# Two token blocks share the first layer's weights in three groups of the inner dimension instead of two, the weights' conversion follows a schedule over the steps, and the short token block comes third

## The chip, the cores and the metric

The program runs on one core of a Trainium2 chip. The metric is the device time of one execution in microseconds; lower is better. The core's engines are named as in the profile: PE multiplies matrices, PEld is its weight load, DVE and ACT do elementwise work, POOL is little used here, and SP issues the DMA transfers.

## The reference

Attention without a softmax (a decaying linear attention), then two feed-forward layers over its 2304 tokens of 512 features.

```python
scores = q @ k.T / sqrt(64)                    # 4 batches, 8 heads, 576 positions, heads of 64
gamma  = 1 - 2 ** (-5 - arange(8))             # per head
ret    = scores * where(i >= j, gamma ** (i - j), 0)
x      = (ret @ v)  -> (2304, 512)
h = x @ w_in;  g = where(h > 0, h, exp(min(h, 0)) - 1);  x = g @ w_out      # layer one, 2048 inner
h = maximum(x @ w_in2, 0);  out = (h * h) @ w_out2                            # layer two, 2048 inner
```

q, k and v are float32; the four weight matrices come as float64 (as pairs of 32-bit words).

## The kernel before

**Tokens and steps.** The 2304 tokens are cut into five blocks (`BLOCKS`, L24), four of 512 and one of 256. The inner dimension of 2048 is cut into 16 slices f of 128. A step is one block and one slice: `up` multiplies the block's x by w_in's slice (12 matmuls into one PSUM tile h), ACT and DVE make g of it, and `down1` or `down2`, called `LAG` = 2 steps later, multiplies g by w_out's slice (12 more for a block of 512, into four PSUM tiles acc). Every product is three matmuls, since each operand is split into an upper and a lower part (`split`, L108; `mm3`, L113). Layer one has 80 steps, layer two 80.

**Groups of layer one.** A block of 512 fills all four acc tiles, so only one block accumulates at a time. Blocks 0 and 1 share layer one's weights in two halves of f (`ORDER1`, L32): block 0 with f 0 to 7, block 1 with f 0 to 7, block 0 with f 8 to 15, block 1 with f 8 to 15. After a first half ACT copies acc out and SP stores it in DRAM (`parts`, L338, L340); at the end it is loaded back and DVE adds it (L322, L330). Then blocks 2 to 4 follow with 16 steps each.

**Attention.** A block's x is made of chunks of at most 128 positions. A chunk has three pieces (`attn_pieces`): transposes of q and k on PE, scores on PE with a mask on DVE (P, L239), values on PE with a split into x by ACT and DVE (L110, L111) and an update of the state st on DVE (L271). Before them DVE scales q and k (L198). Block 0's four chunks stand ahead of the steps; `SPREAD` (L35) says over which steps the pieces of each later block are given out. Block 1 has five chunks.

**Weights.** A unit is one slice of one matrix: 32 units per layer, in the order in which the steps need them (`units`, L362). A unit of layer one is loaded (L129, L134), converted to float32 by two ACT (L144, L145) and four DVE instructions (L146, L147, L148, L151), and split by one ACT and one DVE instruction. Before, `w1_step` (L404) does one unit per piece of block 0's attention and then two per step. Layer two's units are converted in layer one's later steps, parked in DRAM (`park_w`), and fetched and split when block 4 releases layer one's weights.

**What sets the order.** The program is traced in the order of the Python code, but a scheduler with a timeline of its own then fixes the order of the instructions on each engine, as their inputs become ready there. On the chip each engine takes its instructions strictly in that order and waits for semaphores. The SP queue does so too.

Of the kernel before, what the change touches and what calls it, by code (L numbers as in the profile page):

```python
# [14 lines left out]
ALU = mybir.AluOpType  # L15
# [5 lines left out]
KC = DM // P  # L21
NF = DFF // P
TB = 512
BLOCKS = [(0, 512), (512, 512), (1024, 512), (1536, 256), (1792, 512)]  # L24
NB = len(BLOCKS)
LAG = 2
WARM = 3

AHEAD = 6

HALF = NF // 2
ORDER1 = [(b, h * HALF + f) for h in range(2) for b in range(2) for f in range(HALF)]  # L32
ORDER1 += [(b, f) for b in range(2, NB) for f in range(NF)]

SPREAD = {1: (0, HALF - 1), 2: (3 * HALF, 4 * HALF - 1), 3: (2 * NF, 3 * NF - 3), 4: (3 * NF, 4 * NF - 3)}  # L35

MOST = float(np.array([0x7F7FF000 >> 3], np.uint32).view(np.float32)[0])

# [3 lines left out]
def chunks_of_blocks():  # L42


    out = []
    for t, n in BLOCKS:
        end, cs = t + n, []
# [35 lines left out]
def tile_kernel(ctx: ExitStack, tc, q, k, v, w_in1, w_out1, w_in2, w_out2, cst, out):  # L83
    nc = tc.nc
# [15 lines left out]
    parts = dram.tile([2, P, KC, TB], F32, tag="parts", name="parts")  # L100
    w2s = dram.tile([2 * NF, P, DM], F32, tag="w2s", name="w2s")
    x2s = [dram.tile([P, KC, 2, n], F32, tag=f"x2s{i}", name=f"x2s{i}") for i, (_, n) in enumerate(BLOCKS)]
    cs = const.tile([P, C_ALL], F32, name="cs")
# [4 lines left out]
    def split(pair_hi, pair_lo, src, eng=nc.vector):  # L108

        nc.scalar.copy(pair_hi, src)  # L110
        eng.tensor_tensor(out=pair_lo, in0=src, in1=pair_hi.bitcast(F32), op=ALU.subtract)  # L111

    def mm3(ps, l_hi, l_lo, r_hi, r_lo, first, last):  # L113
        nc.tensor.matmul(ps, l_hi, r_hi, start=first, stop=False)  # L114
        nc.tensor.matmul(ps, l_hi, r_lo, start=False, stop=False)  # L115
        nc.tensor.matmul(ps, l_lo, r_hi, start=False, stop=last)  # L116
# [85 lines left out]
    def attn_pieces(ch, blk):  # L202
        b, s, n = ch
        o = b * S + s - BLOCKS[blk][0]
        live = {}
# [77 lines left out]
    def up(layer, blk, f, mid):  # L283
        n = BLOCKS[blk][1]
        x = x_t[layer * NB + blk]
# [20 lines left out]
        split(g[:, 0, :n], g[:, 1, :n], t)  # L306
        g_t[blk, f] = g

    def halves(blk):
        return blk < 2  # L310

    def down1(blk, f):
        n = BLOCKS[blk][1]
        g, w = g_t.pop((blk, f)), w_t[0, 1, f]
        half = halves(blk)
        first, last = f == 0 or half and f == HALF, f == NF - 1 or half and f == HALF - 1
        if first:
            acc_t[blk] = [ps_acc.tile([P, TB], F32, tag="acc", name=f"acc{m}") for m in range(KC)]
        if f == NF - 1 and half:
            back = [raw_p.tile([P, 2, TB], F32, tag="raw", name="part") for _ in range(KC // 2)]  # L320
            for i, t in enumerate(back):
                nc.sync.dma_start(out=t, in_=parts[blk, :, 2 * i:2 * i + 2])  # L322
        for m in range(KC):
            c = slice(m * P, (m + 1) * P)
            a = acc_t[blk][m][:, :n]
            mm3(a, w[:, 0, c], w[:, 1, c], g[:, 0, :n], g[:, 1, :n], first, last)
            if f == NF - 1:
                if half:
                    t = back[m // 2][:, m % 2]
                    nc.vector.tensor_tensor(out=t, in0=a, in1=t, op=ALU.add)  # L330
                    a = t
                x2 = g_p.tile([P, 2, TB], F32R, tag="g", name="x2")[:, :, :n]
                split(x2[:, 0], x2[:, 1], a)
                nc.sync.dma_start(out=x2s[blk][:, m], in_=x2.bitcast(F32))
            elif last:
                if m % 2 == 0:
                    part = raw_p.tile([P, 2, TB], F32, tag="raw", name="part")
                nc.scalar.copy(part[:, m % 2], a)  # L338
                if m % 2:
                    nc.sync.dma_start(out=parts[blk, :, m - 1:m + 1], in_=part)  # L340

    def down2(blk, f):
        t0, n = BLOCKS[blk]
# [19 lines left out]
    w1 = [(0, *u) for u in units]  # L363
    w2 = [(1, *u) for u in units]
# [7 lines left out]
    at = dict(load=0, scale=0, next=0, raw=0, f32=0, split=0, raw2=0, f322=0, park=0, fetch=0, split2=0)  # L372
# [28 lines left out]
            work(todo_[at[name]])  # L401
            at[name] += 1

    def w1_step(n):  # L404

        for _ in range(n):
            while at["raw"] < min(at["f32"] + AHEAD, len(w1)):
                step("raw", 99, w1, lambda u: load_raw(*u))
            step("split", at["f32"], w1, split_w)
            step("f32", at["raw"], w1, to_f32)  # L410
# [3 lines left out]
    first = [attn_pieces(ch, 0) for ch in blocks[0]]  # L414
# [6 lines left out]
    load_next()  # L421
    scale_next()
    scale_next()
    for c, piece in ((0, 0), (1, 0), (0, 1), (1, 1), (0, 2), (2, 0), (1, 2), (3, 0), (2, 1), (3, 1), (2, 2), (3, 2)):
        first[c][piece]()
        w1_step(1)
        if piece == 0 and c < 2:
            scale_next()
        if (c, piece) in ((0, 2), (2, 2)):
            load_next()  # L430
    scale_next()
    at["next"] = len(first)
    steps = [(0, blk, f) for blk, f in ORDER1]
    steps += [(1, blk, f) for blk in range(NB) for f in range(NF)]
    pend = []
    for i, (layer, blk, f) in enumerate(steps):
        def mid():
            for of, (lo, hi) in SPREAD.items():
                if lo <= i < hi:
                    need = 3 * len(blocks[of])  # L440
                    for _ in range((i - lo + 1) * need // (hi - lo) - (i - lo) * need // (hi - lo)):
                        attn_step()
            if at["split"] < len(w1):
                w1_step(2)
            elif layer == 0 and i >= NF and at["f322"] < min(len(w2), (i - NF + 1) * 0.7):

                step("park", at["f322"], w2, park_w)
                with tc.issue_after(mark[0]):
                    step("f322", at["raw2"], w2, to_f32)
                while at["raw2"] < min(len(w2), at["f322"] + 2):  # L450
                    step("raw2", 99, w2, lambda u: load_raw(*u))

        up(layer, blk, f, mid)
        pend.append((layer, blk, f))
        if len(pend) > LAG:
            l, bb, ff = pend.pop(0)
            (down1, down2)[l](bb, ff)
        if at["f322"] == len(w2):
            step("park", 99, w2, park_w)

        j = i - (NB - 1) * NF
        if j >= 0:
            while at["split2"] < len(w2):
                _, which, ff = w2[at["split2"]]
                if ff + (LAG if which else 0) > j:
                    break
                while at["fetch"] < min(at["split2"] + 4, len(w2)):
                    step("fetch", 99, w2, fetch_w)
                step("split2", 99, w2, split_w)

        if (layer, f) == (0, 1) and blk == NB - 1 or (layer, f) == (1, LAG) and blk < NB - 1:
            n = blk + 1 if layer else 0
            new_x(NB + n)
            nc.sync.dma_start(out=x_t[NB + n].bitcast(F32)[:, :, :, :BLOCKS[n][1]], in_=x2s[n])
# [28 lines left out]
```

## Time and profile before

| | |
|---|---|
| median of 3 runs | 934.76 us (933.84 to 935.75) |
| profiled execution | 936.7 us |
| its span, first to last instruction | 934.9 us |
| mean granted PE clock | 0.979 |
| PE busy | 903.4 us (97%), 4934 matmuls |
| DVE busy | 503.0 us (54%) |
| ACT busy | 425.0 us (45%) |
| DMA | 93.27 MB, mean 100 GB/s |

A busy time counts an instruction from its start to its end; on PE, DVE and ACT neighbours overlap, so a stretch in which an engine is called full may still have differing numbers of instructions in it. How far apart two starts are is then the better measure. The granted clock is that of PE, as a share of full speed; it has two levels, 1.2 and 2.4 GHz, and a stretch's mean lies between.

### The profile page before, as it was taken

How to read it: one execution, taken by the hardware profiler on the slowest of the kernel's cores; microseconds unless marked ns; L12 is line 12 of the kernel's file. 1: busy time of each engine (PE TensorE's matmuls, PEld its weight loads, DVE VectorE, ACT ScalarE, POOL GpSimd, SP SyncE). 2: the span in 40 equal slices, each digit the busy share in tenths (PEclk: the TensorE clock that was granted, in tenths of full speed). 3: DMA queues.
4: the chain of work that ended last, by engine and by line, in shares of the span. 5: the costliest groups of instructions: out<-in, count | busy, mean ns of one | idle time of the engine just before them, and what ended most of it. 6: DMA issues, size and time to landing. Idle time of an engine off the chain costs nothing.

```text
span 934.9 us, 12416 instructions
## 1 busy us (share of the span) xinstructions
PE 903.4 (97%) x4934; PEld 751.9 (80%) x4934; DVE 503.0 (54%) x882; ACT 425.0 (45%) x770; POOL 9.3 (1%) x12
## 2 busy tenths in 40 slices
PE   8799679999999999999999999999999999999997
PEld 5677568888787788899888888888888888898886
DVE  5899997367866766788566632222222222323222
ACT  3788554466645555666566632222222222322221
POOL 3000000000000000000000000000000000000000
PEclk9799869999999999999999999999999999999999
DMA  9993621052842833573533520030002001100001
GB/s 233 313 363 80 169 46 23 1 174 90 255 121 72 251 128 96 180 215 103 181 102 102 168 90 1 1 126 9 1 1 90 1 0 60 77 1 22 1 1 45
DMA packets 95929, 93.27 MB, mean 100 GB/s; under 512 B 59136, under 2 KB 77696, under 8 KB 95360
## 3 DMA queue, kind: packets, MB, share of 16 engines
q1 hardware_dynamic: 95872, 92.49, 32.5%
q8 instruction: 38, 0.62, 0.3%
q14 instruction: 19, 0.16, 0.1%
HBM read 67.84 MB, written 24.64 MB: 99 GB/s over the span
## 4 chain that ended last, share of the span: by engine, by line
PE 88%; DVE 9%; DMA 1%; issue 1%; ACT 0%; SPq 0%; DVEq 0%
PE acc L114 14%; PE h L114 14%; PE h L115 13%; PE acc L115 13%; PE h L116 13%; PE acc L116 13%; PE ps_o L255 2%; DVE f L148 1%; PE ps_s L236 1%; DVE f L151 1%; PE ps_o L251 1%; PE ps_t L223 1%; DVE w L111 1%; DVE f L146 1%; DMA v<-in_v_dram 1%
## 5 line engine op out<-in xcount | busy, mean ns | idle before, releaser
L114 PE MATMUL h<-x,w 128*128 128x512 f32 (+1 forms) x640 | 240.3, 376 | 2.8 <-DVE t L301 2.5
L115 PE MATMUL h<-x,w 128*128 128x512 f32 (+1 forms) x640 | 239.1, 374 | 1.2 <-DVE x L111 1.2
L116 PE MATMUL h<-x,w 128*128 128x512 f32 (+1 forms) x640 | 238.1, 372 | 0.0
L305 DVE SCALAR_TENSOR_TENSOR t<-h,t 128x512 f32<-128x512 f32 (+1 forms) x80 | 51.1, 638 | 230.0 <-ACT t L303 230.0
L303 ACT ACTIVATE t<-h 128x512 f32<-128x512 f32 (+1 forms) x80 | 44.4, 555 | 237.2 <-PE h L116 237.2
L114 PEld LDWEIGHTS h<-x,w 128*128 128x128 f32 x640 | 121.9, 191 | 25.6 <-DVE t L301 3.6
L115 PEld LDWEIGHTS h<-x,w 128*128 128x128 f32 x640 | 121.9, 190 | 23.5 <-DVE x L111 2.6
L110 ACT CAST g<-t 128x512 fp32r<-128x512 f32 (+1 forms) x160 | 92.1, 577 | 103.2 <-DVE t L305 52.1
L116 PEld LDWEIGHTS h<-x,w 128*128 128x128 f32 x640 | 122.2, 191 | 20.8
L111 DVE TENSOR_TENSOR g<-t,g 128x512 fp32r<-128x512 f32 (+1 forms) x160 | 101.8, 637 | 65.1 <-ACT g L110 58.6
L115 PE MATMUL acc<-g,w 128*128 128x512 f32 (+1 forms) x320 | 118.4, 371 | 1.1 <-DVE g L111 1.1
L116 PE MATMUL acc<-g,w 128*128 128x512 f32 (+1 forms) x320 | 118.1, 370 | 0.0
L114 PE MATMUL acc<-g,w 128*128 128x512 f32 (+1 forms) x320 | 112.4, 376 | 0.0
L114 PE MATMUL acc<-w,g 128*128 128x512 f32 x288 | 112.3, 390 | 0.0
L115 PE MATMUL acc<-w,g 128*128 128x512 f32 x288 | 112.3, 390 | 0.0
L116 PE MATMUL acc<-w,g 128*128 128x512 f32 x288 | 111.6, 389 | 0.0
L300 DVE SCALAR_TENSOR_TENSOR t<-e,t 128x512 f32<-128x512 f32 (+1 forms) x80 | 50.9, 636 | 57.7 <-ACT t L298 57.3
L296 ACT ACTIVATE t<-h 128x512 f32<-128x512 f32 (+1 forms) x80 | 44.4, 555 | 76.3 <-PE h L116 72.1
L115 PEld LDWEIGHTS acc<-g,w 128*128 128x128 f32 x320 | 60.3, 189 | 11.5 <-DVE g L111 1.6
L114 PEld LDWEIGHTS acc<-g,w 128*128 128x128 f32 x320 | 59.6, 188 | 11.4 <-DVE x L111 0.5
L116 PEld LDWEIGHTS acc<-g,w 128*128 128x128 f32 x320 | 60.3, 188 | 10.2
L116 PEld LDWEIGHTS acc<-w,g 128*128 128x128 f32 x288 | 54.1, 188 | 11.3
(65 smaller groups left out, 922.4 us busy)
## 6 DMA issues: line engine op xcount, KB each, us to landing
raw<-in_moe_w_in_dram SPq DMA_DIRECT2D x32, 512.0 KB, 6.1
raw<-in_moe_w_out_dram SPq DMA_DIRECT2D x32, 512.0 KB, 5.8
w2s<-f SPq DMA_DIRECT2D x32, 256.0 KB, 2.2
x2s<-x SPq DMA_DIRECT2D x16, 512.0 KB, 3.3
f<-w2s SPq DMA_DIRECT2D x32, 256.0 KB, 2.6
x<-x2s SPq DMA_DIRECT2D x4, 2048.0 KB, 7.8
out_dram<-o SPq DMA_DIRECT2D x18, 256.0 KB, 2.7
q<-in_q_dram SPq DMA_DIRECT2D x13, 256.0 KB, 4.9
```

What stands on the lines that cost most here:

```text
L110: nc.scalar.copy(pair_hi, src)
L111: eng.tensor_tensor(out=pair_lo, in0=src, in1=pair_hi.bitcast(F32), op=ALU.subtract)
L114: nc.tensor.matmul(ps, l_hi, r_hi, start=first, stop=False)
L115: nc.tensor.matmul(ps, l_hi, r_lo, start=False, stop=False)
L116: nc.tensor.matmul(ps, l_lo, r_hi, start=False, stop=last)
L146: nc.vector.tensor_scalar_min(a, a, MOST)
L148: nc.vector.scalar_tensor_tensor(out=ai, in0=upper, scalar=-(1 << 31), in1=ai, op0=ALU.bitwise_and, op1=ALU.bitwise_or)
L255: nc.tensor.matmul(ps[e * D:(e + 1) * D, p, :n], vn[:n, 2 * p + e, :], live[e][:n, p, :n], start=not s, stop=True, skip_group_check=True,)
L296: nc.scalar.activation(t, h, AF.Relu, scale=-1.0)
L300: nc.vector.scalar_tensor_tensor(out=t, in0=e, scalar=1.0, in1=t, op0=ALU.add, op1=ALU.mult)
L303: nc.scalar.activation(t, h, AF.Relu)
L305: nc.vector.scalar_tensor_tensor(out=t, in0=h, scalar=0.0, in1=t, op0=ALU.max, op1=ALU.mult)
```

## The change

The short block moves from fourth to third place: block 2 has 256 tokens and two chunks of attention, block 3 has 512 tokens and five chunks. Blocks 0 and 1 go through three groups of f (0 to 5, 6 to 10, 11 to 15) instead of two halves. The middle group adds its sum to the one loaded back and stores it again. `SPREAD` gives block 1's pieces to steps 0 to 4 (before: 0 to 6). `w1_to` takes the number of units that are to be split by then, from the table `EARLY` during block 0's attention and from `units1` at each step, and layer two's conversion starts at step 32 (before: after layer one's, from step 16) at the pace of `units2`.

```diff
--- before.py
+++ after.py
@@ -21,18 +21,34 @@
 KC = DM // P
 NF = DFF // P
 TB = 512
-BLOCKS = [(0, 512), (512, 512), (1024, 512), (1536, 256), (1792, 512)]
+BLOCKS = [(0, 512), (512, 512), (1024, 256), (1280, 512), (1792, 512)]
 NB = len(BLOCKS)
 LAG = 2
 WARM = 3
 
 AHEAD = 6
 
-HALF = NF // 2
-ORDER1 = [(b, h * HALF + f) for h in range(2) for b in range(2) for f in range(HALF)]
+
+GROUPS = ((0, 6), (6, 11), (11, 16))
+ORDER1 = [(b, f) for lo, hi in GROUPS for b in range(2) for f in range(lo, hi)]
+SHARED = len(ORDER1)
 ORDER1 += [(b, f) for b in range(2, NB) for f in range(NF)]
 
-SPREAD = {1: (0, HALF - 1), 2: (3 * HALF, 4 * HALF - 1), 3: (2 * NF, 3 * NF - 3), 4: (3 * NF, 4 * NF - 3)}
+SPREAD = {1: (0, 5), 2: (SHARED - 5, SHARED - 1), 3: (SHARED, SHARED + NF - 2), 4: (SHARED + NF, SHARED + 2 * NF - 2)}
+
+EARLY = (0, 0, 0, 1, 1, 2, 3, 4, 5, 6, 6, 7)
+
+
+def units1(i):
+    return 7 + 1.4 * min(i + 1, 5) + 0.85 * max(i - 4, 0)
+
+
+def units2(i):
+
+    i -= SHARED - 1
+    return 0.6 * min(i, NF) + max(i - NF, 0)
+
+
 
 MOST = float(np.array([0x7F7FF000 >> 3], np.uint32).view(np.float32)[0])
 
@@ -306,17 +322,16 @@
         split(g[:, 0, :n], g[:, 1, :n], t)
         g_t[blk, f] = g
 
-    def halves(blk):
-        return blk < 2
-
     def down1(blk, f):
         n = BLOCKS[blk][1]
         g, w = g_t.pop((blk, f)), w_t[0, 1, f]
-        half = halves(blk)
-        first, last = f == 0 or half and f == HALF, f == NF - 1 or half and f == HALF - 1
+        shared = blk < 2
+        first, last = (any(f == r[e] - (e == 1) for r in (GROUPS if shared else ((0, NF),))) for e in range(2))
         if first:
             acc_t[blk] = [ps_acc.tile([P, TB], F32, tag="acc", name=f"acc{m}") for m in range(KC)]
-        if f == NF - 1 and half:
+
+        more = shared and last and f >= GROUPS[0][1]
+        if more:
             back = [raw_p.tile([P, 2, TB], F32, tag="raw", name="part") for _ in range(KC // 2)]
             for i, t in enumerate(back):
                 nc.sync.dma_start(out=t, in_=parts[blk, :, 2 * i:2 * i + 2])
@@ -324,20 +339,23 @@
             c = slice(m * P, (m + 1) * P)
             a = acc_t[blk][m][:, :n]
             mm3(a, w[:, 0, c], w[:, 1, c], g[:, 0, :n], g[:, 1, :n], first, last)
+            if not last:
+                continue
+            if more:
+                part = back[m // 2]
+                nc.vector.tensor_tensor(out=part[:, m % 2], in0=a, in1=part[:, m % 2], op=ALU.add)
+                a = part[:, m % 2]
             if f == NF - 1:
-                if half:
-                    t = back[m // 2][:, m % 2]
-                    nc.vector.tensor_tensor(out=t, in0=a, in1=t, op=ALU.add)
-                    a = t
                 x2 = g_p.tile([P, 2, TB], F32R, tag="g", name="x2")[:, :, :n]
                 split(x2[:, 0], x2[:, 1], a)
                 nc.sync.dma_start(out=x2s[blk][:, m], in_=x2.bitcast(F32))
-            elif last:
+                continue
+            if not more:
                 if m % 2 == 0:
                     part = raw_p.tile([P, 2, TB], F32, tag="raw", name="part")
                 nc.scalar.copy(part[:, m % 2], a)
-                if m % 2:
-                    nc.sync.dma_start(out=parts[blk, :, m - 1:m + 1], in_=part)
+            if m % 2:
+                nc.sync.dma_start(out=parts[blk, :, m - 1:m + 1], in_=part)
 
     def down2(blk, f):
         t0, n = BLOCKS[blk]
@@ -401,9 +419,9 @@
             work(todo_[at[name]])
             at[name] += 1
 
-    def w1_step(n):
-
-        for _ in range(n):
+    def w1_to(n):
+
+        while at["split"] < min(int(n), len(w1)):
             while at["raw"] < min(at["f32"] + AHEAD, len(w1)):
                 step("raw", 99, w1, lambda u: load_raw(*u))
             step("split", at["f32"], w1, split_w)
@@ -421,9 +439,10 @@
     load_next()
     scale_next()
     scale_next()
-    for c, piece in ((0, 0), (1, 0), (0, 1), (1, 1), (0, 2), (2, 0), (1, 2), (3, 0), (2, 1), (3, 1), (2, 2), (3, 2)):
+    pieces = ((0, 0), (1, 0), (0, 1), (1, 1), (0, 2), (2, 0), (1, 2), (3, 0), (2, 1), (3, 1), (2, 2), (3, 2))
+    for (c, piece), n in zip(pieces, EARLY):
         first[c][piece]()
-        w1_step(1)
+        w1_to(n)
         if piece == 0 and c < 2:
             scale_next()
         if (c, piece) in ((0, 2), (2, 2)):
@@ -441,8 +460,8 @@
                     for _ in range((i - lo + 1) * need // (hi - lo) - (i - lo) * need // (hi - lo)):
                         attn_step()
             if at["split"] < len(w1):
-                w1_step(2)
-            elif layer == 0 and i >= NF and at["f322"] < min(len(w2), (i - NF + 1) * 0.7):
+                w1_to(units1(i))
+            elif layer == 0 and i >= SHARED and at["f322"] < min(len(w2), units2(i)):
 
                 step("park", at["f322"], w2, park_w)
                 with tc.issue_after(mark[0]):
```

The order on the engines, at three places. First DVE, about the last write of block 1's x (the row with x_528 before, x_480 after); w0_12 is the split of slice 12 of w_in, w1_11 that of slice 11 of w_out, f_ a unit in conversion, raw_ its loaded words. Before:

```order
L146 TENSOR_SCALAR f_1175<-f_1175 128x512
L148 SCALAR_TENSOR_TENSOR f_1163<-raw_837,f_1163 128x512
L147 TENSOR_SCALAR f_1175<-f_1175 128x512
L111 TENSOR_TENSOR w0_12_1160<-f_1054,w0_12_1160 128x512
L151 ISA f_1163<-raw_837,f_1163 128x1024
L111 TENSOR_TENSOR x_528<-ps_o_1126,x_528 128x4x64
L148 SCALAR_TENSOR_TENSOR f_1175<-raw_930,f_1175 128x512
L271 TENSOR_TENSOR st_101<-ps_u_1141,st_101 64x4x64 x2
L146 TENSOR_SCALAR f_1222<-f_1222 128x512
L111 TENSOR_TENSOR w1_11_1172<-f_1163,w1_11_1172 128x512
```

After:

```order
L167 ISA f_1490<-raw_1203,f_1490 128x1024
L162 TENSOR_SCALAR f_1537<-f_1537 128x512
L127 TENSOR_TENSOR w1_10_1487<-f_1439,w1_10_1487 128x512
L163 TENSOR_SCALAR f_1537<-f_1537 128x512
L127 TENSOR_TENSOR w0_12_1534<-f_1490,w0_12_1534 128x512
L164 SCALAR_TENSOR_TENSOR f_1537<-raw_1250,f_1537 128x512
L162 TENSOR_SCALAR f_1584<-f_1584 128x512
L127 TENSOR_TENSOR x_480<-ps_o_924,x_480 128x4x64
L167 ISA f_1537<-raw_1250,f_1537 128x1024
L162 TENSOR_SCALAR f_1676<-f_1676 128x512
```

The split of w0_12 stands a few rows ahead of the last x in both; the rows about it are the same kinds of work.

Second PE, where the last attention piece of block 1 (ps_o, ps_u) ends and block 1's first two steps begin (h). Before, with the 96 products of 8 steps of block 0 in `up` and as many in `down1` ahead of it:

```order
L255 MATMUL ps_o<-P_1122,v 64x64
L255 MATMUL ps_o<-P_1120,v 64x64
L255 MATMUL ps_o<-P_1122,v 64x64
L265 MATMUL ps_u<-v,k 64x64 x8
L114 MATMUL h<-x,w_0_189 128x512
L114 MATMUL h<-x,w_1_217 128x512
L115 MATMUL h<-x,w_0_189 128x512
L116 MATMUL h<-x,w_0_189 128x512
```

After, with 72 and 72 of 6 steps ahead of it:

```order
L271 MATMUL ps_o<-P_920,v 64x64
L271 MATMUL ps_o<-P_918,v 64x64
L271 MATMUL ps_o<-P_920,v 64x64
L281 MATMUL ps_u<-v,k 64x64 x8
L130 MATMUL h<-x,w_0_217 128x512
L130 MATMUL h<-x,w_1_269 128x512
L131 MATMUL h<-x,w_0_217 128x512
L132 MATMUL h<-x,w_0_217 128x512
```

The rows are alike; the steps of block 0 in front of them are two fewer.

Third SP, the transfers issued while block 1's attention runs: q_, k_, v_ are inputs of chunks, parts_93 the partial sums in DRAM, raw_16.. units of layer two. Before:

```order
L188 DMA q_910<-in_q_dram 64x8x64
L188 DMA k_912<-in_k_dram 64x8x64
L188 DMA v_914<-in_v_dram 64x8x64
L129 DMA raw_1609<-in_moe2_w_in_dram 128x4x256
L340 DMA parts_93<-part_1356 128x1024
L188 DMA q_1031<-in_q_dram 128x8x64
L340 DMA parts_93<-part_1366 128x1024
L129 DMA raw_1611<-in_moe2_w_in_dram 128x4x256
L134 DMA raw_1655<-in_moe2_w_out_dram 128x1024
L188 DMA k_1033<-in_k_dram 128x8x64
L188 DMA v_1035<-in_v_dram 128x8x64
```

After:

```order
L204 DMA q_619<-in_q_dram 128x8x64
L204 DMA k_621<-in_k_dram 128x8x64
L204 DMA v_623<-in_v_dram 128x8x64
L204 DMA q_716<-in_q_dram 64x8x64
L358 DMA parts_93<-part_1116 128x1024
L358 DMA parts_93<-part_1126 128x1024
L204 DMA k_718<-in_k_dram 64x8x64
L204 DMA v_720<-in_v_dram 64x8x64
L204 DMA q_841<-in_q_dram 128x8x64
L204 DMA k_843<-in_k_dram 128x8x64
```

Two stores of partial sums now stand in front of the k of block 1's last chunk (k_718; k_912 before), and layer two's units are gone from here.

## Rows read from the trace of the kernel before

**Rows 1.** Stretches: busy us (x instructions) by engine, granted clock, DMA share, GB/s.

```profile
core 0: us, PE busy (x) PEld busy (x) DVE busy (x) ACT busy (x) POOL busy (x), PEclk, DMA share, GB/s
...
100.00:120.00 20.00, 10.04 (x95) 8.53 (x94) 19.89 (x40) 10.69 (x20) 0.00 (x0) 0.75 0.68 191
...
125.00:131.00 6.00, 5.69 (x14) 4.51 (x15) 5.96 (x13) 2.60 (x6) 0.00 (x0) 0.54 0.33 70
...
137.00:141.00 4.00, 3.89 (x10) 3.08 (x11) 4.00 (x9) 1.61 (x3) 0.00 (x0) 0.57 0.01 1
...
157.00:200.00 43.00, 43.00 (x204) 35.15 (x203) 21.75 (x35) 24.98 (x43) 0.00 (x0) 1.00 0.09 31
...
280.00:300.00 20.00, 18.82 (x125) 15.40 (x124) 11.10 (x21) 12.05 (x21) 0.00 (x0) 1.00 0.19 49
...
380.00:450.00 70.00, 70.00 (x634) 66.16 (x633) 52.65 (x113) 43.78 (x100) 0.00 (x0) 1.00 0.56 176
```

**Rows 2.** PE's timeline, block 1's attention: start, us, instruction, [idle before it <-releaser].

```profile
119.36 1.97 PE L251 MATMUL ps_o<-qT,st 128*128 128x64 f32 x8 [3.13 <-DVE P L239]
```

**Rows 3.** PE's timeline from block 1's first step on.

```profile
125.31 0.79 PE L115 MATMUL h<-x,w 128*128 128x512 f32 x1 [0.67 <-DVE x L111]
...
125.90 0.63 PE L116 MATMUL h<-x,w 128*128 128x512 f32 x1
...
126.33 0.63 PE L114 MATMUL h<-x,w 128*128 128x512 f32 x1
...
132.88 0.60 PE L223 MATMUL ps_t<-cs,q 128*128 128x128 f32 x4
...
133.32 0.60 PE L223 MATMUL ps_t<-cs,k 128*128 128x128 f32 x4
...
135.25 1.16 PE L236 MATMUL ps_s<-qT,kT 64*128 64x128 f32 x16 [1.34 <-ACT kT L228]
...
137.11 0.61 PE L114 MATMUL h<-x,w 128*128 128x512 f32 x1 [0.69 <-DVE t L301]
...
142.47 1.05 PE L251 MATMUL ps_o<-qT,st 128*128 128x128 f32 x8
...
143.46 1.09 PE L255 MATMUL ps_o<-P,v 128*64 128x128 f32 x16
```

**Rows 4.** DVE's groups by line, 38.2 to 125.3 us: busy us, mean ns, idle.

```profile
L111 DVE TENSOR_TENSOR w<-f,w 128x512 fp32r<-128x512 f32 x21 | 14.2, 683 | 0.1
...
L146 DVE TENSOR_SCALAR f<-f 128x512 f32<-128x512 f32 x21 | 8.8, 418 | 0.0
...
L300 DVE SCALAR_TENSOR_TENSOR t<-e,t 128x512 f32<-128x512 f32 x8 | 5.5, 684 | 1.8 <-ACT t L298 1.8
```

**Rows 5.** DVE's timeline, three neighbours in the full stretch.

```profile
102.46 0.41 DVE L147 TENSOR_SCALAR f<-f 128x512 int32<-128x512 int32 x1
102.79 1.28 DVE L148 SCALAR_TENSOR_TENSOR f<-raw,f 128x512 int32<-128x512 int32 x2
104.00 0.68 DVE L111 TENSOR_TENSOR w<-f,w 128x512 fp32r<-128x512 f32 x1
```

**Rows 6.** DVE's timeline: last x of block 0, DVE's one wait, last x of block 1.

```profile
38.26 0.69 DVE L111 TENSOR_TENSOR x<-ps_o,x 128x512 fp32r<-128x512 f32 x1
...
62.63 0.69 DVE L300 SCALAR_TENSOR_TENSOR t<-e,t 128x512 f32<-128x512 f32 x1 [1.83 <-ACT t L298]
...
124.85 0.41 DVE L111 TENSOR_TENSOR x<-ps_o,x 128x256 fp32r<-128x256 f32 x1
```

**Rows 7.** ACT's timeline: first activation of h in steps 12, 15 and 16.

```profile
156.99 0.60 ACT L296 ACTIVATE t<-h 128x512 f32<-128x512 f32 x1 [3.58 <-PE h L116]
...
174.62 0.60 ACT L296 ACTIVATE t<-h 128x512 f32<-128x512 f32 x1 [1.41 <-PE h L116]
...
180.06 0.60 ACT L296 ACTIVATE t<-h 128x512 f32<-128x512 f32 x1 [1.41 <-PE h L116]
```

**Rows 8.** The page's DMA issues: count, KB each, median us to landing.

```profile
q<-in_q_dram SPq DMA_DIRECT2D x13, 256.0 KB, 4.9
```

## The prediction, made before the changed kernel ran

> **What bounds the kernel now.** I read a table of stretches first, then the timelines of PE, DVE and ACT where a stretch looks odd, then DVE's groups by line. The page calls PE busy nearly throughout; the table of stretches [rows 1] shows two regimes under that. From 157 us on PE is filled at full clock (157:200 and 380:450 have PE 43.00 of 43 and 70.00 of 70 us); only 280:300 loses 1.2 us. A 512-token step takes 5.44 us there, from one activation of h to the next [rows 7], so its 24 matmuls start 0.227 us apart. Before 157 us DVE sets the pace: in 100:120 it works 19.89 of 20 us, PE 10.04, at a granted clock of 0.75. The PE timeline [rows 2] shows the attention of block 1 waiting for DVE's masking (3.13 us for P of its last chunk). The gate is block 1's x: PE cannot finish block 1's first step until DVE has written the last piece of it, at 124.85 us [rows 6]; block 0's last piece was at 38.26. So the kernel is a DVE-bound front and a PE-bound rest, and the change pays by when PE is released, and by how much dense work PE has then done.
>
> **DVE in front of the gate.** DVE's instructions overlap, so their price is the distance of their starts: 0.60 us for 512 columns (two L148 take 102.79 to 104.00), 0.33 for a tensor-scalar [rows 5]. The lines of that stretch [rows 4] show what fills it: 21 weight splits, 21 tensor-scalars of each kind, 8 steps of ELU, and the rest of conversions, scalings and masks. By program order 162 DVE instructions stand after block 0's last x up to block 1's; at these prices 83.7 us, against 86.6 measured (the difference is one wait of 1.83 us for ACT at 62.63 [rows 6] and small ones). In the changed program 154 stand there: the ELU of two steps less (6 instructions, 3.6 us), two scalings less (1.2), one L151 and one tensor-scalar less (0.9), two state updates more (0.8). That is 4.9 us less. The weight splits are 21 in both. The pacing says 14 units by step 4, but the order in which DVE got them is the scheduler's: when block 1's last x comes, the changed DVE has split w0_12, which its steps first read at step 23. So the conversions stay in front of the gate, and it opens at 125.3 - 4.9 = 120.4 us. Bounds: 1.8 us earlier, if the wait for ACT does not recur (the order has other DVE work at hand there); 2 us later, because k of block 1's last chunk is now queued on SP behind two stores of partial sums, which wait for step 5's accumulators, and a load of this kind takes 4.9 us to land in the median [rows 8]. I take neither.
>
> **PE in front of the gate.** Before, block 0 runs 8 steps of its first group before block 1 is needed; now 6. Two steps, 48 matmuls at 0.227 us, 10.9 us of dense work, move from where PE had time to spare to behind the gate. Nothing takes their place: the attention pieces in front are the same, and PE waits for DVE that much longer. This is the main term, +10.9.
>
> **Behind the gate.** Before, PE needs from 125.31 to 156.99, where step 12's activation starts [rows 7], 31.7 us, for 82 dense matmuls (18.6 us) and 5.4 us of attention (by the starts in [rows 3]: four groups of transposes at 0.44, one and a half times scores at 1.1, values at 2.0). So 7.7 us are lost. Of these 4.2 are the slow clock: 12 matmuls start 0.43 us apart instead of 0.227 [rows 3], and 9 more from 137.11 on, the stretches whose mean clocks are 0.54 and 0.57 [rows 1]. The rest is waiting, 1.34 and 0.69 us [rows 3] and little ones, because DVE still has 30 us of work against PE's 24. Now PE has 34.9 us there and DVE 34.6 (64 instructions instead of 56), so PE should wait less. I take 4.0 us lost: 2.4 for the first slow stretch and 1.6 of waits; bounds 0 and 7.7. By program order both engines have done the same work by step 12 in both kernels, so the sum up to there is -4.9 + 10.9 + (4.0 - 7.7) = +2.3 us; with the bounds of the loss -1.7 to +6.0, with those of the gate as well -3.5 to +8.0.
>
> A rule of the Trainium skill speaks on the clock here: "TensorE: Matmul & The Clock Gate", section "HAM oscillation — how this bites in real kernels", says that PE work which follows a long wait begins throttled, and pays for it again after each such wait. This trace agrees (0.43 us a matmul behind the gate). By the rule the longer hole ends in a slow start again and the sum is +2.3; without it the sum would be -0.1.
>
> **The rest of the program.** The third group adds a pass of partial sums per block: 8 DVE adds of 128x512 (8 x 0.60 = 4.8 us) and 4 MB of transfers, in steps 16 to 26, where DVE works 21.75 of 43 us and DMA has a share of 0.09 [rows 1]: nothing; if that cover were gone, at most 4.8 us. Layer two's conversions leave steps 16 to 31; PE was full there, so -0.4 (0 to -1). The short block, now third, carries five chunks of attention and block 1's final sums: 56.7 us of DVE work by the same prices, against 48.6 for the short block before, in a stage that took some 69 us with PE full (in 380:450 [rows 1]). The order crowds it at its start (21 us of DVE against 16 of PE over four steps). In 280:300 PE lost 1.2 us; I take +1.0, bounds 0 and 4, half of the added DVE work. Layer two's products are the same matmuls in another order of blocks: 0.
>
> **The sum.** The profiled execution took 936.7 us, its span 934.9. The change gives +2.3 - 0.4 + 1.0 = +2.9, so 939.6 for an execution like that one. It lies 1.9 above the median of the runs, 934.76; on that scale the forecast is 937.7 us.
>
> **Rivals.** First, the change comes out faster, because the DVE front loses its wait and the hole closes at once. The gate then opens at 118.6, PE runs its 34.9 us without slow clock or waits, and the short block costs nothing: -4.9 - 1.8 + 10.9 - 7.7 - 0.4 = -3.9, about 931 us. For it: PE now has as much work as DVE behind the gate, so DVE can hide. Against it: the clock was low after each hole before, and this hole is longer. It decides where the gate opens early and less than 2 us are lost behind it. Second, no change: 0 to 3 us are lost behind the gate instead of 4, the rest as forecast, 933 to 936.6 us. Third, the pacing does what it says on the engine: 12 units fewer in front of the gate, each 2.5 us of DVE, up to 30 us off the gate, and PE loses little of 20 us: the order of DVE says no, so I count it within the first. Fourth, the short block in third place becomes DVE-bound and its whole +4 is paid, with 7.7 lost behind the gate: -4.9 + 10.9 - 0.4 + 4 = +9.6, 944 us. Against it: 56.7 us of DVE in 69.
>
> **Chances.** Forecast, later by 2 to 6 us: 0.46; its own range is 936.6 to 941. Faster: 0.21. No change: 0.22. The fourth: 0.11. For 8 in 10 the range takes in most of the faster rival and of the fourth: 930.5 to 945. About 0.2% (1.9 us) is what a measurement of this kernel can tell from no change; faster by more 0.21, within 0.22, slower by more 0.57.
>
> **What would show it.** In the profile after: block 1's last x on DVE 4 to 5 us earlier than 124.85; PE idle or slow from about 85 to 121 us, longer than before; step 12's activation near 159 instead of 157, and equal distances from then on. If block 1's last x comes before 116, my count of DVE is wrong; if step 12 is reached before 157, my loss behind the gate is; if steps 32 to 47 show PE waits of several us, the fourth rival is right. Dense steps at other than 5.44 us would overturn all of it.

## The result, and the profile after

The changed kernel takes 945.38 us in the median of 4 runs (942.22 to 946.56); the kernel before, beside it, 935.25 (933.84 to 935.98, 4 runs). The ratio is 1.0105, with a 95% interval of 1.0077 to 1.0133: slower by 10.1 us. The forecast was 937.7, slower by 2.9; the sign was right, the size was not. The profiled execution took 946.56 us, 9.9 more than that of before (936.7).

First the stretches of the kernel after (busy us with the number of instructions by engine, granted clock, DMA share, GB/s), to be read beside [rows 1]:

```profile
core 0: us, PE busy (x) PEld busy (x) DVE busy (x) ACT busy (x) POOL busy (x), PEclk, DMA share, GB/s
80.00:100.00 20.00, 13.28 (x107) 10.10 (x105) 19.93 (x39) 10.36 (x19) 0.00 (x0) 0.89 0.28 86
100.00:117.00 17.00, 10.73 (x105) 9.65 (x105) 16.91 (x34) 8.16 (x15) 0.00 (x0) 0.60 0.23 47
125.00:131.00 6.00, 3.71 (x27) 3.07 (x28) 5.97 (x12) 4.97 (x10) 0.00 (x0) 1.00 0.41 87
...
286.00:301.00 15.00, 12.38 (x98) 11.66 (x97) 12.39 (x23) 5.82 (x12) 0.00 (x0) 0.77 0.83 256
...
287.30:294.20 6.90, 4.28 (x44) 3.85 (x42) 6.90 (x14) 3.84 (x8) 0.00 (x0) 0.95 0.78 205
...
293.50:300.30 6.80, 6.12 (x36) 5.90 (x37) 5.85 (x11) 1.24 (x2) 0.00 (x0) 0.50 0.78 272
...
301.00:350.00 49.00, 49.00 (x468) 45.86 (x468) 38.11 (x88) 30.40 (x74) 0.00 (x0) 1.00 0.64 182
```

and one stretch of the kernel before:

```profile
80.00:100.00 20.00, 18.19 (x123) 14.84 (x122) 19.95 (x39) 13.06 (x23) 0.00 (x0) 1.00 0.06 14
```

Two things stand out. The hole in front of the gate (the start of the last write of block 1's x on DVE) begins earlier: PE works 13.28 of 20 us from 80 on, where it worked 18.19 before. DVE is full all through it. And there is a second hole that the kernel before does not have, at 286 to 301 us, in the first steps of the short block: PE has 98 instructions in 15 us at a mean clock of 0.77, and the DMA share is 0.83. From 293.5 to 300.3 us the clock is at its low level.

The gate and what follows, on DVE (last x of block 0, last x of block 1; compare [rows 6]):

```profile
37.74 0.69 DVE L127 TENSOR_TENSOR x<-ps_o,x 128x512 fp32r<-128x512 f32 x1
...
117.33 0.41 DVE L127 TENSOR_TENSOR x<-ps_o,x 128x256 fp32r<-128x256 f32 x1
```

and on PE (compare [rows 2] and [rows 3]):

```profile
113.12 1.97 PE L267 MATMUL ps_o<-qT,st 128*128 128x64 f32 x8 [2.43 <-DVE P L255]
...
118.39 0.63 PE L132 MATMUL h<-x,w 128*128 128x512 f32 x1
118.82 0.63 PE L130 MATMUL h<-x,w 128*128 128x512 f32 x1
...
119.80 0.39 PE L130 MATMUL h<-x,w 128*128 128x512 f32 x1
120.03 0.39 PE L131 MATMUL h<-x,w 128*128 128x512 f32 x1
...
127.02 1.16 PE L252 MATMUL ps_s<-qT,kT 64*128 64x128 f32 x16 [2.29 <-ACT kT L244]
128.45 0.50 PE L130 MATMUL h<-x,w 128*128 128x512 f32 x1 [0.27 <-DVE t L317]
```

The gate is 7.5 us earlier than before, not 4.9. The first matmuls behind it start 0.43 us apart and from 119.80 on 0.23: four of them meet the low clock, where it was 12 before, and the second slow stretch of before is gone (125:131 is at full clock). The wait for the scores' operands grew instead, from 1.34 to 2.29 us. DVE's groups from 37.7 to 117.7 us (busy us, mean ns; compare [rows 4]) confirm the count of the prediction: as many weight splits and conversions as before, two steps of ELU less.

```profile
L127 DVE TENSOR_TENSOR w<-f,w 128x512 fp32r<-128x512 f32 x21 | 14.3, 685 | 0.0
...
L316 DVE SCALAR_TENSOR_TENSOR t<-e,t 128x512 f32<-128x512 f32 x6 | 4.1, 684 | 0.0
```

ACT's first activations of h in steps 12 ([rows 7]), 24, and 80, the first of layer two:

```profile
158.68 0.60 ACT L312 ACTIVATE t<-h 128x512 f32<-128x512 f32 x1 [2.05 <-PE h L132]
...
225.88 0.60 ACT L312 ACTIVATE t<-h 128x512 f32<-128x512 f32 x1 [0.25 <-PE h L132]
...
543.93 0.60 ACT L319 ACTIVATE t<-h 128x512 f32<-128x512 f32 x1 [1.04 <-PE h L132]
```

The two rows of before that they are to be compared with:

```profile
224.83 0.60 ACT L296 ACTIVATE t<-h 128x512 f32<-128x512 f32 x1 [0.57 <-PE h L116]
...
534.07 0.60 ACT L303 ACTIVATE t<-h 128x512 f32<-128x512 f32 x1 [1.03 <-PE h L116]
```

At step 12 the change has cost 1.7 us (158.68 against 156.99), at step 24 it has cost 1.05, at step 80 9.86. (A dense step takes 5.44 us as before: 176.28 to 181.72 from step 15 to 16.) So the front ended where the forecast put it, and 8.8 us were lost between steps 24 and 80, where the prediction had +0.6.

**The crowd at 286 us.** Rows of the timeline of all engines there:

```profile
282.99 0.34 SPq L337 DMA_DIRECT2D part<-parts  x1
...
287.30 1.29 DVE L346 TENSOR_TENSOR part<-acc,part 128x512 f32<-128x512 f32 x2 [0.96 <-DMA part<-parts]
...
288.02 0.62 ACT L126 CAST x<-part 128x512 fp32r<-128x512 f32 x1 [0.95 <-DVE part L346]
...
289.69 0.67 ACT L160 ACTIVATE raw<-raw 128x512 int32<-128x512 uint32 x1
...
291.29 0.57 ACT L244 COPY kT<-ps_t 128x512 f32<-128x512 f32 x1
...
291.35 0.34 SPq L337 DMA_DIRECT2D part<-parts  x1
...
291.91 1.16 PE L252 MATMUL ps_s<-qT,kT 64*128 64x128 f32 x16 [1.52 <-ACT kT L244]
...
293.11 0.68 DVE L167 CUSTOM_DVE_ANT_0 f<-raw,f 128x1024 uint16<-128x1024 uint16 x1
...
293.71 0.42 DVE L317 TENSOR_TENSOR t<-h,t 128x256 f32<-128x256 f32 x1
...
294.18 0.58 PE L130 MATMUL h<-x,w 128*128 128x256 f32 x1 [1.10 <-DVE t L317]
...
296.48 1.29 DVE L346 TENSOR_TENSOR part<-acc,part 128x512 f32<-128x512 f32 x2 [0.83 <-DMA part<-parts]
297.21 1.26 ACT L126 CAST x<-part 128x512 fp32r<-128x512 f32 x2 [5.34 <-DVE part L346]
```

Block 1's final sums come in two halves. The load of the second is issued 8.4 us after that of the first (291.35 and 282.99), so its adds stand 9.2 us behind the others, and ACT, which takes its instructions in order, waits 5.34 us for them. `part` lives in the three buffers of the pool `raw`, which layer two's loads use from step 32 on as well. SP's waits from 282 to 302 us (us in total, times, longest) show the first half held up by that: its load stands 10.0 us for L167, which reads such a buffer in layer two's conversion.

```profile
SPq L337 <- DVE f L167: 10.0, 1, 10.0
...
SPq L337 <- DVE x L127: 0.8, 1, 0.8
```

The second half's load waits last for DVE's split of the first half, the last to read that half's buffer.

PE, however, waits only twice, 1.52 us until 291.91 for ACT's copy of kT and 1.10 us until 294.18 for DVE's L317, and both waits are over before the second half's adds begin at 296.48. So the late second half is not what PE waits for. In front of these two instructions stand the first half and what crowds about it. DVE waits 0.96 us for that half and is then full from 287.30 to 294.2 (6.90 of 6.90 us), with its adds and splits, the scaling of a chunk and four instructions of layer two's conversion, the last of them (L167) just ahead of L317. ACT waits 0.95 us for the adds, and then its casts and two conversions of layer two (L160, L161) stand ahead of the copy. After PE's waits the clock is at its low level for 6.8 us, which at half speed costs some 3.4 us (an estimate from the row of that stretch), more than the waits themselves. From there to 317 us PE has no further wait of note.

A second, smaller place is at 468 us, in block 4's steps:

```profile
468.48 0.62 ACT L126 CAST w<-f 128x512 fp32r<-128x512 f32 x1 [1.93 <-DMA f<-w2s]
...
472.75 0.50 PE L130 MATMUL h<-x,w 128*128 128x512 f32 x1 [2.07 <-DVE t L317]
```

ACT waits for a parked unit of layer two, the step's ELU stands behind it in ACT's order, and PE waits for the ELU.

### The profile page after: what moved, and what is told of

It reads as the page before. It is cut to its first block, busy times and chain, and to the rows that moved or that the text cites. A ratio compares the mean times of both kernels' runs of the same rounds, so it can differ in the third digit from the quotient of the medians.

```text
span 944.8 us, 12423 instructions
## 1 busy us (share of the span) xinstructions
PE 906.6 (96%) x4934; PEld 753.2 (80%) x4934; DVE 506.9 (54%) x890; ACT 423.3 (45%) x770; POOL 9.3 (1%) x12
## 4 chain that ended last, share of the span: by engine, by line
PE 83%; DVE 12%; DMA 2%; issue 1%; ACT 0%; SPq 0%; POOL 0%; DVEq 0%
PE acc L130 13%; PE acc L131 13%; PE h L130 13%; PE acc L132 13%; PE h L132 13%; PE h L131 13%; DVE f L164 2%; DVE f L167 2%; DVE w L127 2%; PE ps_o L271 2%; PE ps_s L252 1%; DVE f L162 1%; PE ps_o L267 1%; DVE f L163 1%; PE ps_t L239 1%
## 5 line engine op out<-in xcount | busy, mean ns | idle before, releaser
L130 PEld LDWEIGHTS acc<-g,w 128*128 128x128 f32 x320 | 59.3, 188 | 11.6 <-issue 0.9
L132 PEld LDWEIGHTS acc<-g,w 128*128 128x128 f32 x320 | 60.3, 188 | 10.3
L132 PEld LDWEIGHTS acc<-w,g 128*128 128x128 f32 x288 | 54.1, 188 | 11.4
```

## The experiments

**The measure.** In the expectations and here, the loss of a stretch is its length less what its matmuls take at the full clock's start distances (0.227 us for 512 columns, 0.12 for 256, for the small ones of the attention their own distance, at most 0.115). It holds waits and slow clock together; slow attention matmuls count in part as work, so the columns do not add up to the whole difference (8.6 of the 9.9 us at step 80). Stretches run between first activations of h. "Paced" means layer one's units by `EARLY` and `units1`; "late" means layer two's conversion from step 32 by `units2`. All times are medians of the profiled kernel's runs; the ratio is to the runs of the kernel before made beside them. Gate and step 12 are points in time.

| kernel | time, us | ratio (95%) | gate | step 12 | loss to step 12 | 12 to 32 | 32 to 80 |
|---|---|---|---|---|---|---|---|
| before | 935.25 | 1 | 124.8 | 157.0 | 53.0 | 3.5 | 9.1 |
| after | 945.38 | 1.0105 (1.0077 to 1.0133) | 117.3 | 158.7 | 54.1 | 3.2 | 16.9 |
| short_fourth | 937.84 | 1.0029 (1.0017 to 1.0042) | 115.9 | 157.3 | 53.3 | 4.4 | 8.1 |
| two_groups | 938.34 | 1.0022 (1.0008 to 1.0037) | 121.3 | 149.7 | 47.3 | 3.6 | 17.5 |
| paced_on_engine | 936.89 | 1.0021 (1.0004 to 1.0038) | 105.9 | 144.8 | 42.8 | 5.5 | 16.2 |
| w2_as_before | 948.06 | 1.0127 (1.0104 to 1.0149) | 119.6 | 160.9 | 56.4 | 5.4 | 15.6 |
| groups_only | 951.72 | 1.0177 (1.0156 to 1.0199) | 120.7 | 162.0 | 58.9 | 10.3 | 9.1 |
| groups_w2 | 944.97 | 1.0087 (1.0064 to 1.0110) | 120.1 | 162.9 | 58.7 | 4.6 | 11.6 |
| pace_w1_only | 934.57 | 0.9985 (0.9971 to 0.9999) | 121.3 | 149.3 | 46.8 | 6.4 | 10.4 |
| pace_only | 931.13 | 0.9961 (0.9947 to 0.9976) | 121.0 | 149.1 | 46.2 | 5.5 | 7.9 |
| pace_only_binding | 924.09 | 0.9884 (0.9865 to 0.9902) | 109.5 | 138.5 | 37.9 | 5.8 | 10.4 |
| w2_later | 942.61 | 1.0084 (1.0069 to 1.0100) | 117.8 | 159.1 | 54.2 | 3.2 | 13.4 |

**One part undone at a time.** First the short block's place (`short_fourth`; the ranges of blocks 2 to 4 in `SPREAD` go back as well):

```diff
-BLOCKS = [(0, 512), (512, 512), (1024, 256), (1280, 512), (1792, 512)]
+BLOCKS = [(0, 512), (512, 512), (1024, 512), (1536, 256), (1792, 512)]
```

> The changed kernel with one part undone: the short block is fourth again (512, 512, 512, 256, 512 tokens), the three groups and the paces stay. Theory: the crowd of block 1's final sums and five chunks in 256-token steps goes, and with it the slow clock after it: 4 to 5 us less than the changed kernel, 940 to 941 us. Rival (the front and the groups carry the loss): no difference, 945 us.

937.84 us, 7.5 less than after and more than the theory's 4 to 5; the loss from step 32 to 80 falls from 16.9 to 8.1, the rest stays within 1.2 us. The late hole needs the short block's place. The wait for a buffer alone does not make it: in `short_fourth` the first half's load stands 9.0 us on SP for L167 as well, in the kernel before 9.0 us for L151, and in steps 32 to 40 PE waits 1.0 and 1.1 us there, at full clock, for a loss of 3.6 and 4.3 us. That the short steps suffer because each gives PE only half the columns to work on meanwhile is argued, not shown.

Then two halves in place of three groups (`two_groups`; `SPREAD` gives block 1's pieces to steps 0 to 6 and block 2's to 24 to 30), the short block third:

```diff
-GROUPS = ((0, 6), (6, 11), (11, 16))
+GROUPS = ((0, 8), (8, 16))
-    return 7 + 1.4 * min(i + 1, 5) + 0.85 * max(i - 4, 0)
+    return 7 + 1.4 * min(i + 1, 5) + 0.95 * max(i - 4, 0)
```

> The changed kernel with one part undone: two halves of f instead of three groups, block 1's attention given out over steps 0 to 6, the pace after step 5 at 0.95 units a step so that each unit is there in time; the short block stays third. Theory: the front comes back to that of the kernel before, step 12 near 157 us instead of 158.7: 2 us less than the changed kernel, 943 us, and the late waits stay. Rival (the groups carry the loss): 8 to 10 us less, 936 us.

938.34: the rival was nearer. Step 12 comes 9 us earlier than after (149.7), and 7.3 earlier than before: so the pacing gains in front what the groups lose there, and the +1.7 at step 12 is the difference of two terms several times as large. The late loss stays (17.5).

Layer two's conversion from step 16, as before (`w2_as_before`):

```diff
-            elif layer == 0 and i >= SHARED and at["f322"] < min(len(w2), units2(i)):
+            elif layer == 0 and i >= NF and at["f322"] < min(len(w2), (i - NF + 1) * 0.7):
```

> The changed kernel with one part undone: layer two's units are converted from step 16 on at 0.7 a step, as before the change. Theory (the miss lies in two late places): the wait of PE at 470 us, where the fetch of a parked unit comes late while conversions still run in block 4's steps, goes: 2 us less than the changed kernel, 943 to 944 us; the waits in the short block at 290 to 300 us stay or shrink by 1 us, since fewer conversions stand there. Rival (the third group and the front carry the whole loss): no difference to the changed kernel, 945 us. Rival (the late pace hid the conversions well): 1 to 3 us slower, 946 to 948.

948.06, slower still. The wait near 470 us does go, as the theory said (steps 64 to 72 lose nothing instead of 2.3), but steps 32 to 40, where the conversion still runs, lose 8.5. In all it loses 2.2 more from step 12 to 32 and 1.3 less later; the other 2.3, in front of step 12, lie where its order is that of after, with more of the low clock in that execution. So the late conversion is not what made the change slower on balance.

The pacing bound to the engines' order (`paced_on_engine`):

```diff
-                w1_to(units1(i))
+                with tc.issue_after(mark[0]):
+                    w1_to(units1(i))
```

> The changed kernel with the pace made binding: layer one's conversions of a step are ordered behind that step's last ELU activation on ACT, as layer two's are, so that the scheduler can't draw them forward. 14 instead of 24 splits then stand on DVE in front of block 1's last x, 24 us less DVE work by start distances. Theory (conversions drawn forward hold the gate): block 1's last x near 95 us instead of 117, PE lost in front of step 12 falls from 34 to under 18 us: 15 to 20 us less than the changed kernel, 926 to 930 us. Rival (DVE has to do the same work in the end, and PE waits for it later): within 3 us of the changed kernel, 942 to 948 us.

936.89, 8.5 less than after, half of what was expected. 14 units are split in front of the gate instead of 24, as intended, but it opens at 105.9, not near 95: DVE is no longer full in front of it (3.71 of 11 us from 95 to 106).

**One part alone on the kernel before.** The three groups alone (`groups_only`: `GROUPS`, `down1` and block 1's `SPREAD` of the change, the rest as before):

> The kernel before with the three groups alone: the order of the blocks, two units per step and layer two's conversion from step 16 stay as before. Theory (the three groups alone cost about 9 us in front, since two steps of dense work leave the time in which PE waits for DVE; the pacing with two halves reached step 12 at 149.7 us instead of 157.0, and with three groups at 158.7): step 12 near 165 us, time 943 to 945. Rival (the groups cost the 2 to 3 us of the forecast, and the pacing gains little where the groups are three): step 12 near 159, time about 938.

951.72, worse than either expectation. Step 12 is 5.0 us later (theory: 8), and there is a loss of 8.3 us from step 24 to 32 that none had foreseen. DVE's adds and PE's longest wait for one show it:

```profile
237.39 1.29 DVE L346 TENSOR_TENSOR part<-acc,part 128x512 f32<-128x512 f32 x2 [1.33 <-DMA part<-parts]
...
247.04 1.29 DVE L346 TENSOR_TENSOR part<-acc,part 128x512 f32<-128x512 f32 x2 [2.62 <-DMA part<-parts]
...
280.39 0.50 PE L130 MATMUL acc<-g,w 128*128 128x512 f32 x1 [2.29 <-DVE part L346]
```

Again two halves, 9.7 us apart, while layer two's loads, here from step 16 on, share the pool. Here PE does wait for the adds, which free its accumulators: three times, 4.7 us in all, at full clock. Two late halves alone do not make that loss either; the kernel before has them in the same steps, 10 us apart, and PE does not wait there:

```profile
235.06 1.29 DVE L330 TENSOR_TENSOR part<-acc,part 128x512 f32<-128x512 f32 x2 [0.92 <-DMA part<-parts]
...
245.03 1.29 DVE L330 TENSOR_TENSOR part<-acc,part 128x512 f32<-128x512 f32 x2 [1.06 <-DMA part<-parts]
```

`groups_w2` takes layer two's conversion with its loads away from there (the diff of `w2_as_before` the other way round):

> The kernel before with the three groups and, beside them, layer two's conversion only from step 32 at the changed kernel's pace; layer one's units two per step as before, the short block fourth. Theory (with the groups alone, 8.3 us were lost in steps 24 to 32, because the sums loaded back stand behind layer two's loads for the three raw buffers; without those loads the crowd is gone, as it was at steps 32 to 40): the loss in steps 24 to 32 falls to 2 or 3, the time from 951.7 to about 945. Rival (the extra pass of sums costs it by itself, by its adds and transfers): the loss stays near 8, time 950 or more.

944.97, as the theory said; the loss from step 24 to 32 is 3.2. The adds that it has in this stretch wait for PE, and no longer for a transfer:

```profile
225.45 2.05 DVE L346 TENSOR_TENSOR part<-acc,part 128x512 f32<-128x512 f32 x3 [1.36 <-PE acc L132]
...
257.21 1.37 DVE L346 TENSOR_TENSOR part<-acc,part 128x512 f32<-128x512 f32 x2 [2.53 <-PE acc L132]
```

The same test on the changed kernel, four steps later (`w2_later`):

```diff
-            elif layer == 0 and i >= SHARED and at["f322"] < min(len(w2), units2(i)):
+            elif layer == 0 and i >= SHARED + 4 and at["f322"] < min(len(w2), units2(i)):
```

> The changed kernel, but layer two's conversion starts at step 36 instead of 32, so that block 1's final sums do not share the three raw buffers with layer two's loads. Theory (the late partial sums, loaded behind those loads, are what holds ACT and then PE at 287 to 300 us): the loss in steps 32 to 40 falls from 8.2 to 4 or 5 us, time 940 to 942. Rival (the short block's own steps with five chunks of attention are the cause): the loss stays near 8, time 945.

942.61, just above the theory's range. The loss in steps 32 to 40 falls from 8.2 to 2.0, more than expected; steps 48 to 56 and 64 to 72 lose 1.2 and 1.4 more, which fits the same conversions pressing there. The stretch that had the hole; then the last load of the partial sums, and DVE's adds:

```profile
286.00:301.00 15.00, 15.00 (x153) 14.56 (x152) 10.58 (x23) 8.68 (x20) 0.00 (x0) 1.00 0.81 230
```

```profile
257.35 0.66 SPq L337 DMA_DIRECT2D part<-parts  x1
...
280.81 1.88 DVE L346 TENSOR_TENSOR part<-acc,part 128x512 f32<-128x512 f32 x3
282.94 0.68 DVE L346 TENSOR_TENSOR part<-acc,part 128x512 f32<-128x512 f32 x1
```

With the buffers free, the last load is issued 23 us ahead of the adds. All four adds come within 2.8 us and wait for no transfer; PE has 153 instructions in the 15 us instead of 98, at full clock, and no wait of note in steps 32 to 40. The DMA share in these 15 us is 0.81, about as in the changed kernel, so that amount of traffic alone does not hold PE. The edit takes away the loads, which hold the buffers, and the conversion's instructions on ACT and DVE together; which of them counts it does not tell.

**The pacing without groups and short block.** `pace_only` is the changed kernel with two halves (and the 0.95 of `two_groups`) and the short block fourth; `pace_w1_only` has layer two's conversion from step 16 as well; `pace_only_binding` is `pace_only` with the edit of `paced_on_engine`.

> Two halves of the shared steps, the short block fourth as before, but layer one's units and layer two's conversion paced as in the changed kernel. Theory (the pacing gains 7 us in front where two halves are kept, and the late loss is the short block's place): step 12 at 150 us and nothing of note lost from step 32 to 48, time 927 to 930. Rival (what the pacing gains in front is given back later, by layer two's conversion that it moves to the later steps): 934 to 936, with the loss in steps 48 to 72.

> Two halves, the short block fourth, layer two's conversion from step 16 as before: only the pacing of layer one's units is new. Theory (the 4 us that both pacings together gained come from layer one's units, in front): step 12 near 149 us, time 931 to 932. Rival (they come from layer two's conversion that leaves steps 16 to 31): step 12 near 157, time about 935. If both take part, 932 to 934 with step 12 near 149.

`pace_only` takes 931.13, 4.0 less than before (ratio below 1 with its interval), a little above the theory's range: step 12 at 149.1 as expected, 2.0 more lost from 12 to 32. `pace_w1_only` reaches step 12 as early (149.3) and ends at 934.57: it loses 2.9 and 1.3 us more than before in the two later columns. So layer one's pacing makes the gain in front, and it is kept only where layer two's conversion moves too; neither rival is right alone. What the gain in front is made of shows in the stretch up to step 12, first before, then in `pace_only`:

```profile
0.00:157.00 157.00, 131.56 (x891) 104.74 (x892) 137.14 (x259) 100.12 (x180) 9.27 (x12) 0.88 0.67 183
...
0.00:149.10 149.10, 123.24 (x883) 98.04 (x884) 134.47 (x256) 99.44 (x179) 8.91 (x12) 0.92 0.69 185
```

PE is idle as long in both (25.4 and 25.9 us). What falls is the time at the low clock: from the means of 0.88 and 0.92 some 37.7 and 23.9 us, and half of that difference, 6.9 us by this estimate, is about the difference in loss (53.0 and 46.2). So the gain lies in the clock; in what way the new order of DVE's work brings it about, these runs do not show.

> As the one with the pacing alone, but a unit of layer one is also bound to come behind the step before it in the order of the engines: 16 units instead of 24 are split in front of block 1's last x. Theory (DVE's work in front of that x sets the gate): the gate 8 to 12 us earlier than with the pacing alone, the time 4 to 6 us less, 922 to 925. Rival (the latency of the attention's own chain and its loads hold the gate once DVE is no longer full, as the changed kernel with the binding order hinted at): the gate earlier by 5 us or more, the time within 2 us of the pacing alone.

924.09, 11.0 less than before and the fastest of all. The gate is 11.5 us earlier than in `pace_only`, the time 7.0 less: the theory, with a gain beyond its 4 to 6 us. Yet the rival's limit is there as well. In 100:110 DVE works 4.09 of 10 us:

```profile
100.00:110.00 10.00, 7.15 (x98) 6.39 (x98) 4.09 (x9) 1.70 (x4) 0.00 (x0) 0.74 0.40 81
```

and it waits, from 80 to 110 us, for ACT's part of x and for the loads of q and k:

```profile
DVE x L127 <- ACT x L126: 4.0, 2, 2.3
DVE q L214 <- DMA q<-in_q_dram: 2.4, 2, 1.7
DVE k L214 <- DMA k<-in_k_dram: 1.6, 1, 1.6
```

(us in total, times, longest). So what is left to gain in front of the gate would have to come from the attention's own chain and the order of its loads; no run tried it.

## Why the prediction was wrong

**What bounds the kernel: right.** A DVE-full front up to block 1's x and a PE-bound rest; with two halves, binding fewer units in front of the gate moves it by 11.5 us and the time by 7.0.

**The gate: mechanism right, size short.** Forecast 4.9 us earlier, measured 7.5 (PE goes on at 117.94, not at 120.4). The count held (21 splits, ELU of 6 steps), the two stores on SP did no harm (DVE has no wait from 37.7 to 117.7), and the wait for ACT at 62.63 [rows 6] did not recur, which was the bound of 1.8 us that I did not take.

**Two steps of dense work moved behind the gate: right.** From the gate to step 12 it takes 41.35 us against 32.14, +9.2. With the pacing, three groups in place of two halves cost 6.8 and 7.1 us of loss up to step 12 (54.1 against 47.3 with the short block third, 53.3 against 46.2 with it fourth), without it 5.9 (58.9 against 53.0).

**Behind the gate: 4.0 forecast, 6.0 measured** (7.7 before as I counted then, 8.1 from the gate by the measure above). The slow clock was shorter than I took it, the waits longer (2.29 us for kT alone). The stretch from the gate to step 12 was to grow by 7.2 us and grew by 9.2. The two errors, 2.6 us on the gate and 2.0 behind it, mostly cancelled, which is luck; +1.7 at step 12 against +2.3 is therefore better than its parts. What the pacing is worth in front, some 6 us, I had not priced as a term at all: I showed that it takes no unit from in front of the gate, which is right, and concluded that it does little.

**The failed step: "The rest of the program".** It had -0.4 for layer two's conversions leaving steps 16 to 31 and +1.0, at most 4, for the short block in third place, and came to +0.6; measured from step 24 to step 80 it was +8.8. The -0.4 was right (3.2 against 3.5 us lost from step 12 to 32); the term that was mis-sized is the short block's. Its place is worth 7.5 us with three groups and 7.2 with two (938.34 against 931.13). I had set DVE's 56.7 us against 69 us of PE, found cover and charged half of the added DVE work; for waits of PE behind the order on ACT and DVE, and for the clock after them, I put nothing. Over the stage the cover is there, and PE is full at 301 to 350 us. But in steps 32 to 40 the change loses 8.2 us (4.3 before): 2.6 are PE's two waits while DVE is full, some 3.4 the low clock after them, and some 2 are lost without layer two's conversion too (`w2_later`, at full clock and without a wait).

The hole takes two things together, the short block in third place and layer two's conversion with its loads in the same steps. Without the first the loss in steps 32 to 40 is 3.6 us (`short_fourth`), without the second 2.0 (`w2_later`). I priced where the conversions leave and not where they arrive; a sentence of mine had even counted 21 us of DVE against 16 of PE at that place. The fourth rival had the place and nearly the time (944): its DVE-bound block is there for some 7 us and not over the stage, and of its 7.7 us behind the gate 6.0 were lost. Whether the held buffers or the conversion's own instructions on ACT and DVE weigh more was not separated.

**What stays open.** Of the 7.8 us that steps 32 to 80 lose more than before, 3.9 lie in steps 32 to 40 and about as much in steps 40 to 72. There the trace has one wait of PE, the 2.07 us at 472.75; steps 64 to 72 lose 2.3 us with it and next to nothing in `w2_as_before` and in `short_fourth` (-0.1 and 0.2). For the rest, at full clock and in small pieces, no run isolated the cause. `w2_later` returned 3.5 us net. A fourth buffer for the sums was not tried.

## What to carry to other kernels

When a change moves work out of one stage, price the stage it goes into: see which buffers it takes there, what its instructions stand in front of on each engine, and how much work the bottleneck has per step. Here the same conversions and the same shared buffers cost little beside steps of 512 tokens and much beside steps of 256. Before you name the wait that costs the time, compare when the bottleneck's waits end: here a 5.34 us wait of ACT looks like the cause and ends after them. And a wait can cost more than its length, as 2.6 us of waits and 3.4 of slow clock show. A sum near zero made of terms of 5 to 10 us is not a small change: try the parts alone, since here the one good part (the pacing, above all bound to the engines' order) was hidden behind two that cost more than it gave. And a covered total says nothing on the first 15 us of a stage.

## What was not expected of the hardware

The runs of the changed kernel spread with the clock: it took 942.22 us in the run with a mean granted clock of 0.984, and 944.86 to 946.56 in those with 0.977 to 0.979. That is no rule for all: two runs of the kernel before took 933.50 and 937.44 us, both at 0.984. The gate of the four kernels with three groups and the changed pacing lay between 115.9 and 119.6 us. A difference of 2 us in one profile is therefore no finding on this kernel; the 7 us above are.
